# Building float32 weights from float64 words with integer operations, and a smaller feature pool, in a fused attention and MLP kernel

## The chip, the cores and the metric

The kernel runs on one core of a Trainium2 chip. The metric is the device time of one execution in microseconds (us); several runs are given by their median. The engines are TensorE (PE; PEld is its weight load), VectorE (DVE), ScalarE (ACT), GpSimd (POOL) and SyncE (SP), which here issues the DMA transfers. The notes call lines of the kernel `L95` and so on, by the kernel before.

## The reference

Three stages follow one another, on 8 batches of 576 rows with 512 features:

```python
kv = np.einsum('bhsd,bhse->bhde', k, v)                 # linear attention, 8 heads of 64
out = np.einsum('bhsd,bhde->bhse', q, kv)
x = out / np.sqrt(np.mean(out * out, -1, keepdims=True) + 1e-06) * g_norm

u = x + np.real(np.fft.fft(np.fft.fft(x, axis=1), axis=2))   # first MLP
un = (u - mean(u)) / np.sqrt(var(u) + 1e-06)
x = u + np.maximum(un @ w_ch1, 0.0) @ w_ch2                  # 512 -> 2048 -> 512

u = x + (x.T @ U @ V).T                                      # second MLP, rank 32
return u + np.maximum(u @ w_ch1, 0.0) @ w_ch2
```

The weights of both MLPs, and `U` and `V`, come as float64: 8 bytes an element, which the kernel reads as pairs of 32-bit words and turns into float32 on the chip.

## The kernel before

The 4608 rows are cut into 9 blocks of 512 (`NB`), and the 2048 hidden features into 16 groups of 128 (`NF`). One loop at the end of `tile_fused_kernel` runs over `n` from 0 to 287: steps 0 to 143 are the first MLP, 16 steps to a block, steps 144 to 287 the second. A step splits one tile of second-layer weights into a high and a low part (`split_w2`, `L153`, `L154`), does the first layer for one group (`emit_l1`, 12 matmuls, then `gh` on ScalarE and `gl` on VectorE, `L173`, `L174`), splits the first-layer weights of two steps later (`split_w1`, `L145`, `L146`), does the second layer for the group before (`emit_l2`, 12 matmuls), and then runs the side tasks that the table `side[n]` holds for it. The program order of each engine is written by hand in this way (`tc.manual_schedule()`); every engine, and SyncE's queue of transfers, executes in that order.

The side tasks of the first MLP's blocks are the attention, the Fourier transform and the normalisation of the next batch (`batch_tasks`, on all engines), loads, and the conversion of weights. A weight tile is 128x512 float64, loaded by `raw_load` (`L77`) into one of two buffers `raw` as 128x512x2 words: word 0 is the low half `lw`, word 1 the high half `hw` with sign, 11 bits of exponent and 20 of mantissa. `convert` takes a pair of tiles, `conv_a` for each and then `conv_b` for each:

- `conv_a`: VectorE masks the exponent out of `hw` into `pw` (`L85`), ScalarE scales and shifts it to a float32 exponent with `ebias` (`L86`) and scales the low words to float (`L87`), VectorE masks the mantissa with its leading one (`L88`).
- `conv_b`: VectorE puts the sign into `pw` (`L93`), and mantissa and low words together in floating point (`L95`); GpSimd multiplies by `pw` (`L97`).

After a pair, `w_next` issues the loads of the next pair into the two buffers. Three pairs of the first MLP's weights are converted ahead of the loop (two tiles of them one by one), the other 13 in steps 0 to 12 (`w_conv`), one in each. The second MLP's 16 pairs (`w_pre`) go to HBM as float32 and are read back later; they are converted in steps 0, 7 and 9 of blocks 1 to 5 and step 0 of block 6 (`spots`). The tables of `U` and `V` are converted in block 7 (`t_b_tables`), three tiles.

The features of a block are a pair of tiles `xh`, `xl` (high and low part), in pool `pa` for the first MLP, one buffer each, written by `t_tr`. For the second MLP `t_u2` writes them into pool `pb`, two buffers each, from step 10 of the block before. `pb` is opened in block 7 at the place of the attention's pool `at`, which is closed just before.

Of the kernel before, what the change touches and what calls it, by code (L numbers as in the profile page):

```python
# [10 lines left out]
F32 = mybir.dt.float32  # L11
F32R = mybir.dt.float32r
U32 = mybir.dt.uint32
AF = mybir.ActivationFunctionType
ALU = mybir.AluOpType
# [14 lines left out]
BT = 512  # L30
NB = NT // BT
NF = DFF // 128
VPAD = 192
EPS = 1e-6


@with_exitstack
def kernel(ctx: ExitStack, tc: tile.TileContext, qT, kvm, gn, w1a, w2a, w1b, w2b,
                      ucat, v4, tabs, outT):
    nc = tc.nc  # L40
    f32 = lambda ap: ap.bitcast(F32)

    com = ctx.enter_context(tc.tile_pool(name="com", bufs=1))
# [23 lines left out]
    ident = com.tile([128, 128], F32, name="ident")  # L67
    xe0 = com.tile([C, 3, B], F32, name="xe0")
    nhalf = com.tile([128, 8], F32, name="nhalf")
    ebias = com.tile([128, 1], F32, name="ebias")  # L70
    muT = com.tile([128, NT // 128], F32, name="muT")


    def raw_load(src, n):

        r = com.tile([128, 512, 2], U32, tag="raw", name="raw", bufs=2)
        nc.sync.dma_start(out=r[:, 0:n].rearrange("p n w -> p (n w)"), in_=src.bitcast(U32))  # L77
        return r[:, 0:n]

    def conv_a(raw, out):  # L80

        n = raw.shape[1]
        lw, hw = raw[:, :, 0], raw[:, :, 1]
        pw = com.tile([128, 512], U32, tag="cv1", name="cv1", bufs=2)[:, 0:n]
        nc.vector.tensor_scalar(out=pw, in0=hw, scalar1=0x7FF00000, scalar2=None, op0=ALU.bitwise_and)  # L85
        nc.scalar.activation(out=pw, in_=pw, func=AF.Relu, scale=8.0, bias=ebias)  # L86
        nc.scalar.activation(out=f32(lw), in_=lw, func=AF.Copy, scale=2.0 ** -52)  # L87
        nc.vector.tensor_scalar(out=out.bitcast(U32), in0=hw, scalar1=0xFFFFF, scalar2=0x100000,  # L88
                                op0=ALU.bitwise_and, op1=ALU.bitwise_or)
        return raw, out, pw  # L90

    def conv_b(raw, out, pw):
        nc.vector.scalar_tensor_tensor(out=pw, in0=raw[:, :, 1], scalar=0x80000000, in1=pw,  # L93
                                       op0=ALU.bitwise_and, op1=ALU.bitwise_or)
        nc.vector.scalar_tensor_tensor(out=out, in0=out.bitcast(U32), scalar=2.0 ** -20, in1=f32(raw[:, :, 0]),  # L95
                                       op0=ALU.mult, op1=ALU.add)
        nc.gpsimd.tensor_tensor(out=out, in0=out, in1=f32(pw), op=ALU.mult)  # L97

    def convert(*pairs):
        for c in [conv_a(*p) for p in pairs]:  # L100
            conv_b(*c)
# [56 lines left out]
    xt = {}  # L158
# [38 lines left out]
    pa = ctx.enter_context(tc.tile_pool(name="pa", bufs=1))  # L197
# [336 lines left out]
    pbx = {}  # L534
    x2 = {}
    pt = {}

    def t_b_tables(step):
        vw = S + 2 * VPAD
        half = [slice(0, vw // 2), slice(vw // 2, vw)]  # L540
        if step == 0:
            pbx["raw"] = [raw_load(ucat, 10 * RANK), raw_load(v4[:, half[0]], vw // 2)]
        elif step == 1:
            pb = pbx["pb"] = ctx.enter_context(tc.tile_pool(name="pb", bufs=1))
            uf = pb.tile([128, BT], F32, tag="o", name="uf", bufs=4)[:, 0:10 * RANK]
            convert((pbx["raw"].pop(0), uf))
            pbx["raw"].append(raw_load(v4[:, half[1]], vw // 2))
            uf = uf.rearrange("p (k r) -> p k r", r=RANK)
            u1 = pbx["u1"] = pb.tile([128, 10, 4, RANK], F32R, name="u1")
            for k in (0, 2, 3):  # L550
                nc.scalar.activation(out=u1[:, :, k, :], in_=uf, func=AF.Copy)
            nc.vector.tensor_tensor(out=u1[:, :, 1, :], in0=uf, in1=f32(u1[:, :, 0, :]), op=ALU.subtract)
        else:
            pb, c = pbx["pb"], half[step - 2]
            if step == 2:
                pbx["vs"] = pb.tile([128, vw], F32R, name="vs")
            vs = pbx["vs"]
            vf = pb.tile([128, BT], F32, tag="o", name="vf", bufs=4)[:, 0:vw // 2]
            convert((pbx["raw"].pop(0), vf))
            nc.scalar.activation(out=vs[:, c], in_=vf, func=AF.Copy)  # L560
            nc.vector.tensor_tensor(out=vs[96:128, c], in0=vf[96:128], in1=f32(vs[96:128, c]), op=ALU.subtract)
# [44 lines left out]
    def t_u2(j, dc):  # L606
        pb = pbx["pb"]
        blk = NB + j
        if dc == 0:
            xt[blk] = (pb.tile([128, 4, BT], F32R, tag="xh", name=f"xhb{j}", bufs=2),  # L610
                       pb.tile([128, 4, BT], F32R, tag="xl", name=f"xlb{j}", bufs=2))
        xh, xl = xt[blk]
        cols = slice(128 * dc, 128 * dc + 128)
        ps = side_bank(f"u2_{j}_{dc}")
# [60 lines left out]
    with tc.manual_schedule():  # L675
# [2 lines left out]
        nc.vector.memset(kvbd, 0.0)  # L678
        nc.vector.memset(f32(e288), 0.0)
        nc.scalar.activation(out=e288, in_=f32(e288), func=AF.Copy)  # L680
        nc.vector.memset(ebias, -896.0 * 2.0 ** 23)
        load_kv(0)
        load_q(0)
        nc.sync.dma_start(out=gnb, in_=gn)
# [33 lines left out]
        load_kv(1)  # L718
        t_s1(0, 0, 0)
        cv = [conv_a(raws.pop(0), w_new(0))]  # L720
        t_s1(0, 0, 1)
        t_s1(0, 1, 0)
        t_s1(0, 1, 1)
        conv_b(*cv[0])
        t_s2(0, 0)
        cv.append(conv_a(raws.pop(1), w_new(1)))
# [53 lines left out]
        for n in range(2 * NA):  # L780
            i, j = n % NF, n // NF
# [108 lines left out]
```

## Time and profile before

| | |
|---|---|
| runs | 1943.33 us (median of 3, 1941.99 to 1943.92) |
| the profiled execution | 1941.54 us, span 1939.7 us |
| PE busy | 1828.6 us, 94% |
| VectorE, ScalarE, GpSimd busy | 1000.8, 779.9, 769.0 us |
| TensorE's granted clock, mean | 0.976 |
| read from HBM, written | 102.88 MB, 36.73 MB |

The span runs from the first instruction to the last on the core. Busy times of different engines overlap. PE is full in the second half, so the place to look is the first: which engine PE waits for there, and what that engine does meanwhile. The chain of waits is followed back from the end: it shows in each moment one instruction or transfer without which the next could not have begun.

### The profile page before, as it was taken

What the parts mean: (1) busy time and instruction counts of PE and PEld (TensorE: products, weight loads), DVE (VectorE), ACT (ScalarE), POOL (GpSimd) and SP (SyncE); (2) the same over time, 40 slices, a digit from 0 to 9 for tenths busy, and PEclk for the clock granted to TensorE, in tenths of its full rate; (3) what the DMA queues carried; (4) which work ended last, traced back from release to release, by engine and by line L of the source; (5) the groups of instructions that cost most, each with busy time, mean ns of one, the idle gap of its engine ahead of it and who ended that gap; (6) DMA issues with size and microseconds to landing.
All of it is one profiled execution on the core that took longest, in us unless ns stands there. A gap on an engine that the chain in (4) does not pass through costs nothing.

```text
span 1939.7 us, 22822 instructions
## 1 busy us (share of the span) xinstructions
PE 1828.6 (94%) x8520; PEld 1509.4 (78%) x8520; DVE 1000.8 (52%) x1526; ACT 779.9 (40%) x1462; POOL 769.0 (40%) x592
## 2 busy tenths in 40 slices
PE   4667889999999999999999999999999999999999
PEld 3556778778787878878888888888888888888887
DVE  5898785766668576665443333333333333333222
ACT  4444443444434444433434343433343333333332
POOL 4586565544546554444322222232222222222322
PEclk7788999999999999999999999999999999999999
DMA  4524415133241513302222301010101010100000
GB/s 158 185 88 173 159 48 209 55 141 127 88 137 47 210 55 141 105 1 90 72 89 92 108 1 50 1 44 1 49 0 44 1 50 1 44 1 22 1 22 22
DMA packets 61760, 142.14 MB, mean 73 GB/s; under 512 B 11129, under 2 KB 13898, under 8 KB 58834
## 3 DMA queue, kind: packets, MB, share of 16 engines
q1 hardware_dynamic: 61650, 140.69, 20.9%
q8 instruction: 67, 1.10, 0.2%
q14 instruction: 43, 0.35, 0.1%
HBM read 102.88 MB, written 36.73 MB: 72 GB/s over the span
## 4 chain that ended last, share of the span: by engine, by line
PE 74%; DVE 13%; POOL 6%; issue 3%; ACT 3%; DMA 2%; SPq 0%; DVEq 0%; POOLq 0%; ACTq 0%
PE h L168 11%; PE h L170 11%; PE h L169 11%; PE acc L193 7%; PE acc L194 7%; PE acc L192 7%; PE acc L188 4%; PE acc L190 4%; PE acc L189 4%; POOL ss L269 2%; POOL x L282 2%; DVE f L301 2%; PE kv L244 2%; DVE eh L330 1%; DMA raw<-in_w2a 1%
## 5 line engine op out<-in xcount | busy, mean ns | idle before, releaser
L146 POOL TENSOR_TENSOR w1l<-w,w1h 128x512 fp32r<-128x512 f32 x274 | 357.0, 1303 | 972.1 <-ACT w1h L145 948.9
L174 DVE SCALAR_TENSOR_TENSOR gl<-h,gh 128x512 fp32r<-128x512 f32 x288 | 198.2, 688 | 392.4 <-ACT gh L173 392.2
L173 ACT ACTIVATE gh<-h 128x512 fp32r<-128x512 f32 x288 | 171.0, 594 | 501.8 <-PE h L170 501.7
L154 DVE TENSOR_TENSOR w2l<-w,w2h 128x512 fp32r<-128x512 f32 x283 | 208.7, 738 | 188.6 <-ACT w2h L153 187.8
L188 PE MATMUL acc<-w2h,gl 128*128 128x512 f32 x576 | 235.0, 408 | 47.4 <-DVE gl L174 47.4
L153 ACT ACTIVATE w2h<-w 128x512 fp32r<-128x512 f32 x288 | 180.9, 628 | 160.7 <-PE acc L194 113.0
L189 PE MATMUL acc<-w2l,gh 128*128 128x512 f32 x576 | 231.3, 402 | 6.6 <-POOL w2l L154 6.6
L168 PE MATMUL h<-xl,w1h 128*128 128x512 f32 x576 | 230.3, 400 | 1.4 <-DVE xl L492 1.4
L168 PE MATMUL h<-xlb,w1h 128*128 128x512 f32 x576 | 231.1, 401 | 0.0
L190 PE MATMUL acc<-w2h,gh 128*128 128x512 f32 x576 | 230.7, 401 | 0.0
L170 PE MATMUL h<-xh,w1l 128*128 128x512 f32 x576 | 226.4, 393 | 2.2 <-POOL w1l L146 2.2
L170 PE MATMUL h<-xhb,w1l 128*128 128x512 f32 x576 | 228.3, 396 | 0.0
L169 PE MATMUL h<-xhb,w1h 128*128 128x512 f32 x576 | 228.1, 396 | 0.0
L169 PE MATMUL h<-xh,w1h 128*128 128x512 f32 x576 | 225.9, 392 | 0.0
L194 PE MATMUL acc<-gh,w2h 128*128 128x512 f32 x576 | 225.4, 391 | 0.0
L193 PE MATMUL acc<-gl,w2h 128*128 128x512 f32 x576 | 225.4, 391 | 0.0
L192 PE MATMUL acc<-gh,w2l 128*128 128x512 f32 x576 | 224.7, 390 | 0.0
L145 ACT ACTIVATE w1h<-w 128x512 fp32r<-128x512 f32 x288 | 179.5, 623 | 22.9 <-POOL w L97 22.9
L188 PEld LDWEIGHTS acc<-w2h,gl 128*128 128x128 f32 x576 | 111.8, 194 | 80.0 <-DVE gl L174 57.4
L189 PEld LDWEIGHTS acc<-w2l,gh 128*128 128x128 f32 x576 | 112.2, 195 | 30.7 <-POOL w2l L154 8.2
L190 PEld LDWEIGHTS acc<-w2h,gh 128*128 128x128 f32 x576 | 112.0, 194 | 24.3
L170 PEld LDWEIGHTS h<-xh,w1l 128*128 128x128 f32 x576 | 109.2, 190 | 26.5 <-POOL w1l L146 2.6
(167 smaller groups left out, 2824.4 us busy)
## 6 DMA issues: line engine op xcount, KB each, us to landing
kv<-in_kvm SPq DMA_DIRECT2D x14, 1280.0 KB, 8.3
q<-in_qT SPq DMA_DIRECT2D x8, 1220.0 KB, 7.8
x_d<-x2o SPq DMA_DIRECT2D x36, 256.0 KB, 2.1
x2f<-x_d SPq DMA_DIRECT2D x36, 256.0 KB, 3.7
outT<-o SPq DMA_DIRECT2D x36, 256.0 KB, 2.0
raw<-in_w1a SPq DMA_DIRECT2D x16, 512.0 KB, 9.7
raw<-in_w2a SPq DMA_DIRECT2D x16, 512.0 KB, 3.5
u_d<-x SPq DMA_DIRECT2D x32, 256.0 KB, 2.6
```

The costliest lines, as they stand in the source:

```text
L146: (nc.vector if n in on_dve else nc.gpsimd).tensor_tensor(out=al, in0=a, in1=f32(ah), op=ALU.subtract)
L154: (nc.gpsimd if n in CLP else nc.vector).tensor_tensor(out=cl, in0=c, in1=f32(ch), op=ALU.subtract)
L168: nc.tensor.matmul(out=h, lhsT=ah[:, kc, :], rhs=xl[:, kc, :], start=(kc == 0), stop=False)
L169: nc.tensor.matmul(out=h, lhsT=ah[:, kc, :], rhs=xh[:, kc, :], start=False, stop=False)
L170: nc.tensor.matmul(out=h, lhsT=al[:, kc, :], rhs=xh[:, kc, :], start=False, stop=(kc == 3))
L174: nc.vector.scalar_tensor_tensor(out=gl, in0=h, scalar=0.0, in1=f32(gh), op0=ALU.max, op1=ALU.subtract)
L188: nc.tensor.matmul(out=a, lhsT=gl[:, tt], rhs=ch, start=s, stop=False)
L189: nc.tensor.matmul(out=a, lhsT=gh[:, tt], rhs=cl, start=False, stop=False)
L190: nc.tensor.matmul(out=a, lhsT=gh[:, tt], rhs=ch, start=False, stop=e)
L192: nc.tensor.matmul(out=a, lhsT=cl[:, tt], rhs=gh, start=s, stop=False)
L193: nc.tensor.matmul(out=a, lhsT=ch[:, tt], rhs=gl, start=False, stop=False)
L194: nc.tensor.matmul(out=a, lhsT=ch[:, tt], rhs=gh, start=False, stop=e)
```

## The change

`conv_a` and `conv_b` are rewritten. ScalarE now begins: it takes the absolute value of `hw`, read as a float32 (`Abs`), into `pw`; VectorE clamps it to the range that float32 can hold (`HMIN`, `HMAX`); ScalarE scales the low words by 2^-29 and writes them back as integers; VectorE shifts `pw` left by 3 and masks it, which gives exponent and upper mantissa bits of the result. `conv_b` is one VectorE instruction, which puts sign and top exponent bit of `hw` and the low words together, and an integer add on GpSimd in the multiply's place. The floating-point step `L95`, the constant `ebias` and its memset are gone.

The features of the second MLP's block `j` come from `x_new`: for odd `j` the tiles `xh`, `xl` of `pa`, for even `j` one buffer in `pb`, where the pair of block 0 is now the first thing allocated.

```diff
--- before.py
+++ after.py
@@ -33,6 +33,8 @@
 VPAD = 192
 EPS = 1e-6
 
+HMIN, HMAX = (float(v) for v in np.array([0x38000000, 0x47EFFFFF], np.uint32).view(np.float32))
+
 
 @with_exitstack
 def tile_fused_kernel(ctx: ExitStack, tc: tile.TileContext, qT, kvm, gn, w1a, w2a, w1b, w2b,
@@ -67,7 +69,6 @@
     ident = com.tile([128, 128], F32, name="ident")
     xe0 = com.tile([C, 3, B], F32, name="xe0")
     nhalf = com.tile([128, 8], F32, name="nhalf")
-    ebias = com.tile([128, 1], F32, name="ebias")
     muT = com.tile([128, NT // 128], F32, name="muT")
 
 
@@ -79,22 +80,22 @@
 
     def conv_a(raw, out):
 
+
+
         n = raw.shape[1]
         lw, hw = raw[:, :, 0], raw[:, :, 1]
         pw = com.tile([128, 512], U32, tag="cv1", name="cv1", bufs=2)[:, 0:n]
-        nc.vector.tensor_scalar(out=pw, in0=hw, scalar1=0x7FF00000, scalar2=None, op0=ALU.bitwise_and)
-        nc.scalar.activation(out=pw, in_=pw, func=AF.Relu, scale=8.0, bias=ebias)
-        nc.scalar.activation(out=f32(lw), in_=lw, func=AF.Copy, scale=2.0 ** -52)
-        nc.vector.tensor_scalar(out=out.bitcast(U32), in0=hw, scalar1=0xFFFFF, scalar2=0x100000,
-                                op0=ALU.bitwise_and, op1=ALU.bitwise_or)
+        nc.scalar.activation(out=f32(pw), in_=f32(hw), func=AF.Abs)
+        nc.vector.tensor_scalar(out=f32(pw), in0=f32(pw), scalar1=HMIN, scalar2=HMAX, op0=ALU.max, op1=ALU.min)
+        nc.scalar.activation(out=lw, in_=lw, func=AF.Copy, scale=2.0 ** -29)
+        nc.vector.tensor_scalar(out=out.bitcast(U32), in0=pw, scalar1=3, scalar2=0x3FFFFFF8,
+                                op0=ALU.logical_shift_left, op1=ALU.bitwise_and)
         return raw, out, pw
 
     def conv_b(raw, out, pw):
-        nc.vector.scalar_tensor_tensor(out=pw, in0=raw[:, :, 1], scalar=0x80000000, in1=pw,
+        nc.vector.scalar_tensor_tensor(out=pw, in0=raw[:, :, 1], scalar=0xC0000000, in1=raw[:, :, 0],
                                        op0=ALU.bitwise_and, op1=ALU.bitwise_or)
-        nc.vector.scalar_tensor_tensor(out=out, in0=out.bitcast(U32), scalar=2.0 ** -20, in1=f32(raw[:, :, 0]),
-                                       op0=ALU.mult, op1=ALU.add)
-        nc.gpsimd.tensor_tensor(out=out, in0=out, in1=f32(pw), op=ALU.mult)
+        nc.gpsimd.tensor_tensor(out=out.bitcast(U32), in0=out.bitcast(U32), in1=pw, op=ALU.add)
 
     def convert(*pairs):
         for c in [conv_a(*p) for p in pairs]:
@@ -535,6 +536,10 @@
     x2 = {}
     pt = {}
 
+    def x_new(j):
+        pool = pa if j % 2 else pbx["pb"]
+        return tuple(pool.tile([128, 4, BT], F32R, tag=t, name=f"{t}b{j}") for t in ("xh", "xl"))
+
     def t_b_tables(step):
         vw = S + 2 * VPAD
         half = [slice(0, vw // 2), slice(vw // 2, vw)]
@@ -542,6 +547,7 @@
             pbx["raw"] = [raw_load(ucat, 10 * RANK), raw_load(v4[:, half[0]], vw // 2)]
         elif step == 1:
             pb = pbx["pb"] = ctx.enter_context(tc.tile_pool(name="pb", bufs=1))
+            xt[NB] = x_new(0)
             uf = pb.tile([128, BT], F32, tag="o", name="uf", bufs=4)[:, 0:10 * RANK]
             convert((pbx["raw"].pop(0), uf))
             pbx["raw"].append(raw_load(v4[:, half[1]], vw // 2))
@@ -606,9 +612,8 @@
     def t_u2(j, dc):
         pb = pbx["pb"]
         blk = NB + j
-        if dc == 0:
-            xt[blk] = (pb.tile([128, 4, BT], F32R, tag="xh", name=f"xhb{j}", bufs=2),
-                       pb.tile([128, 4, BT], F32R, tag="xl", name=f"xlb{j}", bufs=2))
+        if dc == 0 and j:
+            xt[blk] = x_new(j)
         xh, xl = xt[blk]
         cols = slice(128 * dc, 128 * dc + 128)
         ps = side_bank(f"u2_{j}_{dc}")
@@ -678,7 +683,6 @@
         nc.vector.memset(kvbd, 0.0)
         nc.vector.memset(f32(e288), 0.0)
         nc.scalar.activation(out=e288, in_=f32(e288), func=AF.Copy)
-        nc.vector.memset(ebias, -896.0 * 2.0 ** 23)
         load_kv(0)
         load_q(0)
         nc.sync.dma_start(out=gnb, in_=gn)
```

On VectorE, at step 0 of block 0, the first pair of the loop reads before (`w2l` and `gl` are the step's low parts, `cv` is `pw`, `w` the result):

```order
L95 SCALAR_TENSOR_TENSOR w_0_2_594<-w_0_2_594,raw 128x512
L154 TENSOR_TENSOR w2l_616<-w_0_0_415,w2h_615 128x512
L174 SCALAR_TENSOR_TENSOR gl_633<-h_619,gh_632 128x512
L85 TENSOR_SCALAR cv_642<-raw 128x512
L88 TENSOR_SCALAR w_0_3_640<-raw 128x512
L85 TENSOR_SCALAR cv_647<-raw 128x512
L88 TENSOR_SCALAR w_0_3_641<-raw 128x512
L93 SCALAR_TENSOR_TENSOR cv_642<-raw,cv_642 128x512
L95 SCALAR_TENSOR_TENSOR w_0_3_640<-w_0_3_640,raw 128x512
L93 SCALAR_TENSOR_TENSOR cv_647<-raw,cv_647 128x512
L95 SCALAR_TENSOR_TENSOR w_0_3_641<-w_0_3_641,raw 128x512
L154 TENSOR_TENSOR w2l_663<-w_0_1_485,w2h_662 128x512
```

and with the change, on the same engine at the same place:

```order
L155 TENSOR_TENSOR w2l_608<-w_0_0_412,w2h_607 128x512
L175 SCALAR_TENSOR_TENSOR gl_625<-h_611,gh_624 128x512
L89 TENSOR_SCALAR cv_634<-cv_634 128x512
L91 TENSOR_SCALAR w_0_3_632<-cv_634 128x512
L89 TENSOR_SCALAR cv_639<-cv_639 128x512
L91 TENSOR_SCALAR w_0_3_633<-cv_639 128x512
L96 SCALAR_TENSOR_TENSOR cv_634<-raw 128x512
L96 SCALAR_TENSOR_TENSOR cv_639<-raw 128x512
L155 TENSOR_TENSOR w2l_653<-w_0_1_481,w2h_652 128x512
```

The pair has six instructions in place of eight; the first of each tile now reads `cv`, ScalarE's result, and no longer `raw`.

On ScalarE, at the same place, before:

```order
L153 ACTIVATE w2h_615<-w_0_0_415 128x512
L173 ACTIVATE gh_632<-h_619 128x512
L145 ACTIVATE w1h_636<-w_0_2_593 128x512
L86 ACTIVATE cv_642<-cv_642,ebias 128x512
L87 ACTIVATE raw<-raw 128x512
L86 ACTIVATE cv_647<-cv_647,ebias 128x512
L153 ACTIVATE w2h_662<-w_0_1_485 128x512
```

and with the change:

```order
L154 ACTIVATE w2h_607<-w_0_0_412 128x512
L174 ACTIVATE gh_624<-h_611 128x512
L146 ACTIVATE w1h_628<-w_0_2_587 128x512
L88 ACTIVATE cv_634<-raw 128x512
L90 ACTIVATE raw<-raw 128x512
L88 ACTIVATE cv_639<-raw 128x512
L154 ACTIVATE w2h_652<-w_0_1_481 128x512
```

The places are the same; the first activation of each tile reads `raw`, the loaded words, where it read VectorE's result, and it stands behind `gh` and `w1h` in the queue. On GpSimd, SyncE and PE the order is the same row for row.

## Rows read from the trace of the kernel before

**Rows 1.** The page's first line
```profile
span 1939.7 us, 22822 instructions
```

**Rows 2.** Stretches: us, length, then busy time of each engine, clock, DMA
```profile
84.00:240.00 156.00, 120.60 (x534) 95.85 (x533) 132.19 (x194) 72.36 (x136) 108.55 (x72) 0.90 0.40 140
130.00:140.00 10.00, 4.35 (x11) 2.83 (x10) 8.39 (x9) 5.13 (x9) 6.56 (x6) 0.67 0.33 105
240.00:900.00 660.00, 632.80 (x3167) 533.43 (x3166) 451.11 (x700) 285.64 (x570) 344.00 (x270) 0.99 0.30 105
300.00:350.00 50.00, 50.00 (x266) 42.62 (x265) 29.48 (x49) 17.93 (x34) 22.67 (x23) 1.00 0.43 149
900.00:1939.70 1039.70, 1035.83 (x4597) 844.08 (x4595) 357.99 (x532) 386.43 (x674) 277.50 (x216) 1.00 0.10 34
```

**Rows 3.** PE's waits from 240 to 900 us: total, times, longest
```profile
PE acc L188 <- DVE gl L174: 27.2, 14, 2.3
```

**Rows 4.** The chain from 44 to 240 us: shares by line; start, length
```profile
by line: DMA raw<-in_w2a 13.0%; DVE w L95 10.9%; issue 9.9%; DVE cv L93 5.4%; DVE cv L85 5.1%; POOL w L97 4.6%; POOL x L282 4.3%; DVE eh L330 2.9%; POOL ss L269 2.8%; POOL x L383 2.4%; PE tr L487 2.3%; DVE w L88 2.3%; DVE f L301 2.3%; DVE g
...
64.09 1.67 DVE w L95
...
198.96 1.67 DVE w L95
```

**Rows 5.** The conversion by tile and by line: ns min/median/max, first and last start
```profile
L85 DVE TENSOR_SCALAR cv<-raw x67: 399/420/1510, 44.9 to 957.9; 128x512 uint32<-128x512 uint32 x64, 128x480 uint32<-128x480 uint32 x2, 128x320 uint32<-128x320 uint32 x1
L86 ACT ACTIVATE cv<-cv,ebias x67: 563/723/729, 45.9 to 958.3; 128x512 uint32<-128x512 uint32 x64, 128x480 uint32<-128x480 uint32 x2, 128x320 uint32<-128x320 uint32 x1
L93 DVE SCALAR_TENSOR_TENSOR cv<-raw,cv x67: 492/682/1224, 48.6 to 959.7; 128x512 uint32<-128x512 uint32 x64, 128x480 uint32<-128x480 uint32 x2, 128x320 uint32<-128x320 uint32 x1
L97 POOL TENSOR_TENSOR w<-w,cv x32: 1259/1642/2881, 50.0 to 221.1; 128x512 f32<-128x512 f32 x32
...
L95 DVE SCALAR_TENSOR_TENSOR w<-w,raw x32: 673/685/1785, 49.2 to 219.2; 128x512 f32<-128x512 uint32 x32
```

**Rows 6.** VectorE in order of time: start, length
```profile
97.33 1.77 DVE L95 SCALAR_TENSOR_TENSOR w<-w,raw 128x512 f32<-128x512 uint32 x1
...
108.71 1.75 DVE L154 TENSOR_TENSOR w2l<-w,w2h 128x512 fp32r<-128x512 f32 x1
...
114.92 0.42 DVE L85 TENSOR_SCALAR cv<-raw 128x512 uint32<-128x512 uint32 x1
...
117.47 0.68 DVE L93 SCALAR_TENSOR_TENSOR cv<-raw,cv 128x512 uint32<-128x512 uint32 x1
118.08 0.68 DVE L95 SCALAR_TENSOR_TENSOR w<-w,raw 128x512 f32<-128x512 uint32 x1
```

**Rows 7.** GpSimd in order of time, the same stretch
```profile
97.05 1.50 POOL L97 TENSOR_TENSOR w<-w,cv 128x512 f32<-128x512 f32 x1
...
113.23 7.25 POOL L282 TENSOR_TENSOR x<-x,gnb 128x512 f32<-128x512 f32 x2
```

**Rows 8.** Who subtracts for w2l from 84 to 240 us
```profile
L154 DVE TENSOR_TENSOR w2l<-w,w2h x11: 676/679/1745, 90.3 to 237.5; 128x512 fp32r<-128x512 f32 x11
```

**Rows 9.** The chain at the start of block 1
```profile
246.48 0.39 DVE wpre L95
...
247.68 0.75 DVE wpre L95
248.43 0.86 issue
```

**Rows 10.** Who waits around the tile of the exponents: us, times
```profile
  ACT cv L86: 63.6, 42
...
  DVE cv L93: 4.7, 4
```

**Rows 11.** Two other GpSimd operations: ns min/median/max
```profile
L637 POOL TENSOR_TENSOR o<-xhb,xlb x36: 1274/1287/1752, 1161.8 to 1923.0; 128x512 f32<-128x512 f32 x36
...
L269 POOL TENSOR_TENSOR ss<-ss,nhalf x40: 1629/1918/2158, 17.0 to 828.5; 128x8 f32<-128x8 f32 x32, 98x8 f32<-98x8 f32 x8
```

## The prediction

> **What bounds the kernel now.** I read the stretches first. From 900 us on PE is busy 1035.8 of 1039.7 us at full clock, so nothing the other engines save there can show; between 240 and 900 us it stands idle for 27 us, between 84 and 240 us (the first MLP's block 0) for 35 us, and there the granted clock averages 0.90 [rows 2]. The waits say for whom: between 240 and 900 us the second layer's first matmul waits 14 times for `gl` from VectorE, 27.2 us, which is all of that idle time [rows 3]. So VectorE's place in the step is what can be bought. The chain from 44 to 240 us then says which VectorE work: `L95`, the last step of the weight conversion, holds 10.9% of 196 us, 21.4 us, more than any other instruction; the multiply after it on GpSimd (`L97`) holds 4.6%, 9.0 us; the loads of raw words hold 13.0%, 25 us [rows 4]. The conversions left for block 0 are 13 pairs, one in each of the steps 0 to 12.
>
> What one conversion costs: `L85` and `L88` 0.42 us each, `L93` 0.68, `L95` 0.685 at the median but 1.785 at worst, `L97` 1.64 at the median and 1.26 at best [rows 5]. The stretched ones explain themselves in the order of time. The second `L95` of a pair takes 1.77 us where it starts 0.28 us behind `L97`, and so does a `w2l` subtraction (1.75) that stands there instead [rows 6, 7]. The other way round, eight conversion instructions from 114.92 us on run at 0.42 and 0.68 us while two GpSimd multiplies beside them take 7.25 us [rows 6, 7]. So these instructions exclude one another: what one engine gives up, the other can use.
>
> **What the change takes out.** 67 instructions `L95`, one per conversion, and nothing comes in their place: the exponent is now put together by shifts and an integer add. VectorE's busy time should fall by at least 67 x 0.685, 46 us, and by more for the stretched ones; only a part of that is on the path.
>
> *Block 0 and the start.* All of `L95`'s 21.4 us on the chain is the upper end. Seven of its pieces there are stretched ones, about 1.7 us each (the first and the last in [rows 4]), some 1.08 above 0.60, the pitch at which two such instructions follow each other (117.47 and 118.08 us [rows 6]). That excess belongs to the multiply, which still runs, and meets whatever comes next. In block 0 this is a `w2l` subtraction on VectorE in 11 of 16 steps [rows 8], which is excluded too; in the other 5 GpSimd makes `w2l` itself and VectorE goes on with `gl` out of PSUM. So 11/16 of 7 x 1.08, 5.2 us, is only handed on: 21.4 - 5.2 = **16.2 us**, lower end 21.4 - 7.6 = 13.8.
>
> The Trainium skill (SBUF — State Buffer, Who interferes with whom) calls this pair of ports an exclusive lock that the first comer keeps for its whole instruction. By that rule every stretched piece is handed on and the sum takes 13.8; the trace agrees where VectorE is late [rows 6], but shows GpSimd stretched far beyond one VectorE instruction [rows 7], so the order of issue does not settle it.
>
> *GpSimd.* The integer add is not in the trace. Nearest is the float add of the same tile, 1.287 us [rows 11]; farthest is the power, 1.918 us for 8 columns, which shows that an operation of another kind can cost a multiple per element [rows 11]. I take 1.29. With one excluded VectorE instruction fewer, `L97`'s 9.0 us on the chain shrink by 1 - 1.29/1.64: **1.9 us**, lower end 0.
>
> *Blocks 1 to 6.* Each has a pair (second MLP's weights) in its first step, where VectorE has just caught up with PE: in block 1 `L95` holds 0.39 and 0.75 us of the chain, and 0.86 us of issue stands behind [rows 9]. Then follow normalisation, folds and the idle PE. I take two pitches of 0.60, 1.2 us a block, 6 x 1.2 = **7.2 us**; ends 1.14 and 2.0, 6.8 and 12 us. The other ten of these pairs stand at steps 7 and 9, where PE is busy 50 of 50 us [rows 2]: 0. The conversions of the tables lie behind 900 us: 0, and if that cover went, 3 x 0.7 us.
>
> **What it moves.** Before, VectorE began a conversion as soon as the words had landed, and ScalarE waited for it. Now ScalarE begins (absolute value) and VectorE's clamp waits. Behind that clamp stand `w2l` and `gl`, and behind them PE. ScalarE is the early one today: it waited 63.6 us in 42 places for `L85`, and VectorE 4.7 us in 4 for ScalarE [rows 10]. Where the words come last, VectorE starts one activation later (`L86`, 0.72 us [rows 5]), but no longer waits for it in the middle. I charge **1.5 us**; the ends are 0 and 0.6 us for each of 19 pairs, 11 us. The clamp, the shift and the new OR are priced like `L85`, `L88` and `L93`, the same kinds on the same widths; if the clamp ran like `L93`, 0.26 us more, 19 pairs would lose 10 us, which lies inside the range. Order and number of instructions on GpSimd, SyncE and PE are unchanged; each raw load waits for the last reader of its buffer, now the OR, one instruction earlier.
>
> *The pools.* Odd blocks' features of the second MLP go to the first MLP's buffers, whose last reader is block 8, eleven steps before the first write; two buffers still alternate. Dropping `ebias` takes one memset away. Both: 0, covered by the saturated PE [rows 2].
>
> **Sum.** 16.2 + 1.9 + 7.2 - 1.5 = 23.8 us. The profiled execution took 1941.54 us for its span of 1939.7 [rows 1]; 1941.5 - 23.8 = 1917.7, and the median of the runs lies 1.8 above that execution: **1919 us**. What is late next is the raw loads, 25 us of the chain, which stay.
>
> **Rivals.**
> 1. *The integer add is slow.* GpSimd runs it by another loop. A pair frees two VectorE slots of 0.6 us; an add longer than 1.29 + 0.6 = 1.9 us takes them back, and from there the kernel is slower. At 2.6 us, twice the float add, a pair loses 1.4 us: 19 x 1.4 = 27 us, of which GpSimd's idle third in block 0 (108.5 busy of 156 [rows 2]) hides 9: 1961. For it: the power's price [rows 11], and no integer add in the trace. Against it: all 128x512 two-input operations on GpSimd cost about 1.26 to 1.29 at best, whatever the operation [rows 5, 11]. Chance 0.09. The Trainium skill (GPSIMD Engine Reference, Engine selection) says only that such an add is done natively and exactly, and gives no price.
> 2. *The new wait eats it.* ScalarE's queue is in order, and the absolute value stands behind `gh` and the high parts, which wait for PE and GpSimd. If that makes the clamp late by 0.6 us in each of 19 pairs, and the raw loads hold the chain in a third of block 0 (5 of the 16 us), the gain is 23.8 - 10 - 5, some 8 us: 1935; with the clamp's worse price, nothing. For it: 13% of raw loads on the chain [rows 4]. Against: 63.6 against 4.7 us [rows 10]. Chance 0.14, of which 0.06 ends within 0.2%.
> 3. *More comes back.* If all stretched pieces go, 21.4 + 1.9 + 12, and the clock of block 0 rises: it is 0.90 over 156 us, 0.67 (between the levels of 1.2 and 2.4 GHz) where PE works 4.35 of 10 us, and 1.00 where it is always busy [rows 2], so a busier PE may get back some of the 16 us that 0.10 lacks: 40 us and more, 1900 or below. For it: PE idles 62 us from 84 to 900 us. Against: the loads, and that GpSimd is nearly as full as VectorE. Chance 0.06.
>
> **The numbers.** Forecast 0.71: a gain of 10 us (13.8 + 0 + 6.8 - 11) to 35 us (21.4 + 1.9 + 12 - 0), 1908 to 1933. The range leaves out most of rivals 1 and 3 and the end of rival 2: 1899 to 1940. A measurement tells 0.2%, 4 us, from no change. Faster 0.71 + 0.06 + 0.08 = 0.85; same 0.06, and 0.01 from rival 1; slower 0.08.
>
> **What would show it.** Right: VectorE's busy time down by 46 us or more; the new OR at 0.68 us and hardly stretched, `w2l` stretched more often; the add at 1.3 us or a little above; the wait for `gl` between 240 and 900 us at about 20 instead of 27 us; block 8 reached some 24 us earlier, and the same time from there to the end. Wrong: the add near 2 us or more; long waits of the clamp for ScalarE; the clamp at 0.7 us; or PE idle in block 0 as before, with the raw loads in `L95`'s place on the chain.

## The result

The changed kernel takes **1920.11 us** (median of 4 runs, 1918.78 to 1920.98); the kernel before took 1942.66 us beside it (4 runs, 1941.12 to 1943.92). The ratio is 0.9884, with an interval of 0.9867 to 0.9901: 1.2% faster, 22.5 us, where the prediction said 1919 us. The profiled execution took 1920.98 us for a span of 1919.2, 20.6 us less than the one of before. The total came out within 1 us; two of its terms did not, and a third that was put at nothing had a value. They are taken apart below.

The page of the kernel after, its first lines (busy us, share of the span, instructions):

```profile
span 1919.2 us, 22748 instructions
## 1 busy us (share of the span) xinstructions
PE 1816.7 (95%) x8520; PEld 1504.9 (78%) x8520; DVE 966.8 (50%) x1458; ACT 773.9 (40%) x1462; POOL 751.5 (39%) x592
```

VectorE is busy 34 us less than before (1000.8), not 46 or more: what `L95` gave up, other instructions took over in part; `w2l` alone went from 208.7 to 231.8 us. The stretches, cut where block 0 and the long stall now end (us, length; busy time of PE, PEld, DVE, ACT, POOL; granted clock, DMA share, GB/s), against [rows 2]:

```profile
84.00:228.80 144.80, 116.42 (x533) 93.98 (x532) 116.92 (x166) 69.67 (x136) 96.09 (x70) 0.91 0.41 148
228.80:900.00 671.20, 644.74 (x3235) 542.51 (x3234) 447.69 (x682) 286.95 (x579) 341.73 (x272) 0.99 0.30 104
900.00:1919.20 1019.20, 1014.67 (x4522) 830.98 (x4520) 346.37 (x514) 380.56 (x665) 273.84 (x214) 1.00 0.10 34
```

Block 0 and the start are shorter, PE idles in the blocks from 1 on for about as long as before (26.5 us), and behind 900 us, where nothing should have changed, PE is as full as ever and the stretch is 20.5 us shorter. Of these 15.3 are only that block 7 begins sooner (900.1 us instead of 915.4); the other 5 are a gain of that stretch itself.

The conversion by tile and line (ns min/median/max, first and last start; then who waited around that tile), against [rows 5, 10]. `L88` is the absolute value, `L89` the clamp, `L91` the shift, `L96` the OR, `L98` the integer add:

```profile
L88 ACT ACTIVATE cv<-raw x67: 490/666/708, 45.1 to 942.3; 128x512 f32<-128x512 f32 x64, 128x480 f32<-128x480 f32 x2, 128x320 f32<-128x320 f32 x1
L89 DVE TENSOR_SCALAR cv<-cv x67: 407/428/1519, 45.8 to 943.0; 128x512 f32<-128x512 f32 x64, 128x480 f32<-128x480 f32 x2, 128x320 f32<-128x320 f32 x1
L96 DVE SCALAR_TENSOR_TENSOR cv<-raw x67: 493/684/1121, 48.1 to 944.7; 128x512 uint32<-128x512 uint32 x64, 128x480 uint32<-128x480 uint32 x2, 128x320 uint32<-128x320 uint32 x1
...
L98 POOL TENSOR_TENSOR w<-w,cv x32: 1259/1660/1751, 48.8 to 208.7; 128x512 uint32<-128x512 uint32 x32
...
  ACT w1h L146: 35.5, 14
...
  DVE cv L89: 19.5, 23
```

Each instruction costs what its neighbour in the old trace cost: the integer add 1.26 us at best and 1.66 at the median, the multiply 1.26 and 1.64. The wait is new: VectorE's clamp waited for ScalarE 23 times, 19.5 us, where its waits around this tile had been 4.7 us in 4.

And the excess of a pair, some 1.08 us on VectorE beside GpSimd's operation, went on to the next instruction. VectorE at the start of block 1, in order of time (start, length), in the kernel after:

```profile
232.20 0.42 DVE L89 TENSOR_SCALAR cv<-cv 128x512 f32<-128x512 f32 x1
232.65 0.43 DVE L91 TENSOR_SCALAR wpre<-cv 128x512 uint32<-128x512 uint32 x1
233.00 0.42 DVE L89 TENSOR_SCALAR cv<-cv 128x512 f32<-128x512 f32 x1
233.45 0.43 DVE L91 TENSOR_SCALAR wpre<-cv 128x512 uint32<-128x512 uint32 x1
233.80 1.29 DVE L96 SCALAR_TENSOR_TENSOR cv<-raw 128x512 uint32<-128x512 uint32 x2
235.00 1.76 DVE L155 TENSOR_TENSOR w2l<-w,w2h 128x512 fp32r<-128x512 f32 x1
236.68 0.68 DVE L175 SCALAR_TENSOR_TENSOR gl<-h,gh 128x512 fp32r<-128x512 f32 x1
```

and the same place before:

```profile
244.44 0.42 DVE L85 TENSOR_SCALAR cv<-raw 128x512 uint32<-128x512 uint32 x1
244.78 0.42 DVE L88 TENSOR_SCALAR wpre<-raw 128x512 uint32<-128x512 uint32 x1
...
247.60 1.76 DVE L95 SCALAR_TENSOR_TENSOR wpre<-wpre,raw 128x512 f32<-128x512 uint32 x1
249.29 0.68 DVE L154 TENSOR_TENSOR w2l<-w,w2h 128x512 fp32r<-128x512 f32 x1
```

Before, the stretched instruction was `L95` (1.76 us) and `w2l` behind it ran at 0.68; now `w2l` is stretched to 1.76. From the pair's first instruction to `gl` it is 4.48 us instead of 5.45 (`gl` started at 249.89): 0.97 us saved.

Where the time went, from the starts of each block's first `gl` in the traces (us; 80.7 and 82.0 are the first of all; "odd" are blocks 1, 3, 5, 7 of the second MLP, whose features went to the first MLP's pair, "even" its blocks 0, 2, 4, 6):

```
                before   after  gain   predicted
to step 0         82.0    80.7   1.3   } 17.1
block 0          159.1   148.1  11.0   }
blocks 1-6       674.3   671.2   3.1     6.7
blocks 7-8       182.8   182.8   0.0     0
2nd MLP, odd     374.6   369.2   5.4     0
2nd MLP, even    377.9   377.5   0.4     0
last block+end    89.0    89.7  -0.6     0
```

(The predicted 1.5 us for the wait is split here by its 13 and 6 pairs.) In this pair of traces block 0 and the start gave 5 us less than forecast, blocks 1 to 6 gave 3.6 less, and the second MLP's blocks gave 6 that nobody had counted. The first of these is the least certain, as experiment 2 will show.

### The profile page after: what moved, and what is told of

It reads as the page before. It is cut to its first block, busy times and chain, and to the rows that moved or that the text cites. A ratio compares the mean times of both kernels' runs of the same rounds, so it can differ in the third digit from the quotient of the medians.

```text
span 1919.2 us, 22748 instructions
## 1 busy us (share of the span) xinstructions
PE 1816.7 (95%) x8520; PEld 1504.9 (78%) x8520; DVE 966.8 (50%) x1458; ACT 773.9 (40%) x1462; POOL 751.5 (39%) x592
## 4 chain that ended last, share of the span: by engine, by line
PE 81%; DVE 9%; POOL 4%; ACT 3%; issue 2%; DMA 1%; SPq 0%; DVEq 0%; POOLq 0%; ACTq 0%
PE h L169 12%; PE h L171 12%; PE h L170 12%; PE acc L195 7%; PE acc L194 7%; PE acc L193 7%; PE acc L189 5%; PE acc L191 5%; PE acc L190 5%; DVE f L302 2%; PE kv L245 2%; DVE eh L331 1%; POOL ss L270 1%; PE o L263 1%; PE pt L603 1%
## 5 line engine op out<-in xcount | busy, mean ns | idle before, releaser
L155 DVE TENSOR_TENSOR w2l<-w,w2h 128x512 fp32r<-128x512 f32 x283 | 231.8, 819 | 188.6 <-ACT w2h L154 187.8
L146 ACT ACTIVATE w1h<-w 128x512 fp32r<-128x512 f32 x288 | 179.9, 625 | 35.5 <-POOL w L98 35.5
L169 PEld LDWEIGHTS h<-xlb,w1h 128*128 128x128 f32 x576 | 108.3, 188 | 25.5 <-issue 2.6
```

Source lines behind the costliest of these rows:

```text
L155: (nc.gpsimd if n in CLP else nc.vector).tensor_tensor(out=cl, in0=c, in1=f32(ch), op=ALU.subtract)
L169: nc.tensor.matmul(out=h, lhsT=ah[:, kc, :], rhs=xl[:, kc, :], start=(kc == 0), stop=False)
```

## The experiments

The theory after the result: (a) the pools are worth the 5.8 us, by the place of the features and nothing else; (b) in block 0 the change frees more than was forecast, and the new wait for ScalarE takes back several times the 1.5 us charged. Rivals: the 5.8 us come from the conversion or from a displaced table; and block 0 falls short because the add holds VectorE up as long as the multiply did.

**1. The new conversion with the old pools.**

```diff
-            xt[NB] = x_new(0)
...
-        if dc == 0 and j:
-            xt[blk] = x_new(j)
+        if dc == 0:
+            xt[blk] = (pb.tile([128, 4, BT], F32R, tag="xh", name=f"xhb{j}", bufs=2),
+                       pb.tile([128, 4, BT], F32R, tag="xl", name=f"xlb{j}", bufs=2))
```

> The changed kernel with the pools of the kernel before (both feature pairs of the second MLP in pb). Theory 'place': the 6 us that the changed kernel gained behind step 144 come from where the features lie, and the conversion alone is worth what block 0 and blocks 1 to 6 show, 15 us: 1926 us, and all blocks of the second MLP take 94.5 us again, with a first-layer matmul every 234 ns. Rival 'conversion': the gain behind step 144 has to do with the conversion or the clock, and the pools are worth nothing, as I forecast: 1920 us, odd blocks 93.1 us.

Measured: 1926.39 us (1923.58 to 1927.19), ratio 0.9916 (0.9901 to 0.993). The odd blocks take 374.6 us again, as before the change.

**2. The old conversion with the new pools**, the opposite half.

> The kernel before with the changed pools alone. Theory 'place': 1942.7 - 5.9 = 1937 us; blocks j = 1, 3, 5, 7 of the second MLP 93.1 us at 227 ns a first-layer matmul, the even ones 94.4 at 234, the first MLP unchanged. Rival 'conversion': 1942.7 us, all blocks 94.5.

Measured: 1936.47 us, ratio 0.997 (0.9961 to 0.9979). The odd blocks take 369.2 us as in the full change, and blocks 1 to 6 stay at 673.9. The halves add up: 16.3 us and 6.2 us, together the 22.5 of the change. The conversion has nothing to do with the second MLP's gain.

Block 0 executes the instructions of the kernel before, and yet took 161.9 us where it had taken 159.1. PE worked longer at a lower granted clock, in the old trace and in this one (columns as above):

```profile
82.00:241.10 159.10, 123.70 (x551) 98.55 (x550) 133.30 (x197) 73.67 (x139) 110.55 (x73) 0.90 0.41 140
82.10:244.00 161.90, 126.21 (x544) 99.95 (x544) 131.93 (x197) 73.91 (x139) 111.31 (x73) 0.87 0.40 138
```

So one trace of block 0 is good to some 3 us: with the old conversion it ends at 241.1 and 244.0 us, with the new one (the change and experiments 1, 3 and 4) between 227.7 and 229.5. What block 0 and the start fell short by is 1 to 5.5 us, according to the pair of traces; by the medians of experiment 1, 16.3 us where 23.8 were forecast, less the 3.6 of blocks 1 to 6, it is about 4, an estimate.

The trace shows what differs in the second MLP. Three matmuls of one step, kernel after, in an odd block (start, length; the first is one of the first layer's, the second is the second layer's first, the third comes three matmuls behind that):

```profile
1199.93 0.39 PE L171 MATMUL h<-xhb,w1l 128*128 128x512 f32 x1
...
1201.52 0.39 PE L193 MATMUL acc<-gh,w2l 128*128 128x512 f32 x1
...
1202.20 0.39 PE L193 MATMUL acc<-gh,w2l 128*128 128x512 f32 x1
```

and in an even one:

```profile
1299.90 0.39 PE L171 MATMUL h<-xhb,w1l 128*128 128x512 f32 x1
...
1301.54 0.39 PE L193 MATMUL acc<-gh,w2l 128*128 128x512 f32 x1
...
1302.24 0.39 PE L193 MATMUL acc<-gh,w2l 128*128 128x512 f32 x1
```

From the first row's start to the second's it is seven matmuls: 1.59 us, 227 ns each, and 1.64 us, 234 ns each. Both blocks run at full clock with PE hardly ever idle, and the instructions are the same. What differs is where the 512 columns are read from: by the built program's allocation the pair of the odd blocks lies at bytes 106400 to 122784 of a partition, that of the even blocks from byte 143424 up (before, both pairs from 191328 up). An odd block gained 1.36 us, four of them the 5.4 us in the table. Not all of it falls on the matmuls that read the features: in the median of its steps the twelve first-layer matmuls went from 2.806 to 2.749 us, which is 0.9 us in 16 steps, and the second layer's start right behind them was late as well (0.70 instead of 0.68 us for three matmuls in the rows above), though it reads `gh` and `gl` at the same bytes in both blocks. Why the delay runs on into them no run here shows.

**3. The even blocks' pair put low as well**: the high parts in the four buffers of `un` (up to byte 130976) and the low parts in the two of `raw`, none of which is used any more by then. `Cols` lets the rest of the kernel address such pieces as one tile. All else is as in the change.

```diff
+        return (Cols([pa.tile([128, BT], F32R, tag="un", name=f"xhb{j}_{t}", bufs=4) for t in range(4)], 1),
+                Cols([com.tile([128, 2, BT], F32R, tag="raw", name=f"xlb{j}_{t}", bufs=2) for t in range(2)], 2))
```

> The changed kernel with the even pair in two other places that are idle in the second MLP: xh in the four buffers of the first MLP's rows (bytes 122784 to 130976 of a partition by the allocation), xl in the two buffers of raw words (4000 to 12192). Theory 'low bytes': a feature tile is read slower where it lies high in the partition, with a border between 122784 and 143424; all blocks of the second MLP then run at 227 ns, j = 0, 2, 4, 6 take 93.1 instead of 94.4 us and j = 8 79.2 instead of 80.4: 1920.1 - 6.5 = 1913.6 us. Rival 'neighbours': what matters is whether the pair shares the pool with the tiles that are written and read meanwhile, or that one pair stands apart from the other; then nothing or part of it comes: 1917 to 1920.

Measured: **1911.44 us** (1910.13 to 1912.96), ratio 0.9839 (0.9823 to 0.9855), the fastest version with the whole computation in this study. The four even blocks take 372.2 us instead of 377.5, the odd ones 368.8, and the last block, even too, 78.9 instead of 80.4. The page says it in one line, PE's busy time down by 7 us with as many matmuls:

```profile
PE 1809.5 (95%) x8520; PEld 1504.4 (79%) x8520; DVE 967.4 (51%) x1458; ACT 774.1 (41%) x1462; POOL 752.7 (39%) x592
```

**4. The opposite: the first pair moved up**, by allocating `pa`'s other tiles ahead of it, so that it lies at bytes 127040 to 143424, its low parts from 135232.

> The changed kernel with the same tiles in pool pa, in another order: rows, residuals and outputs first, so that the first pair moves from bytes 106400 to 122784 up to 127040 to 143424 (xh to 135232, xl above). Theory 'low bytes' with a border at 131072: matmuls on xl take 234 ns each in all blocks, those on the last two quarters of xh too, those on its first quarter 227; blocks 7 and 8 of the first MLP and the odd blocks of the second lose 0.9 to 1 us each, the stalled blocks less: 1926 to 1931 us. Rival 'neighbours' (the pool and its other tiles matter, not the bytes): 227 ns as before, 1920 us.

Measured, one run: 1929.35 us. Blocks 7 and 8 of the first MLP, whose features no other edit of this study moved, go from 182.8 to 185.8 us, and the odd blocks back to 374.6: 234 ns for each first-layer matmul. So it is not the pool and not the second MLP, but the place within the partition. Nor is it the alignment: before the change all of this lay 32 bytes higher, `xh` at byte 106432, and blocks 7 and 8 took 182.8 us there too, though 106432 is a multiple of 64 and not of 128, as the slow 127040 and 143424 are. Places up to byte 130976 (experiment 3) are fast, a pair that reaches from 127040 to 143424 is slow, and so is all that was tried higher up. If there is one border, it lies between 127040 and 143424; which part of this pair is already slow the timing does not tell.

**5. Without the absolute value**: the clamp reads the loaded words, sign included.

```diff
-        nc.scalar.activation(out=f32(pw), in_=f32(hw), func=AF.Abs)
-        nc.vector.tensor_scalar(out=f32(pw), in0=f32(pw), scalar1=HMIN, scalar2=HMAX, op0=ALU.max, op1=ALU.min)
+        nc.vector.tensor_scalar(out=f32(pw), in0=f32(hw), scalar1=HMIN, scalar2=HMAX, op0=ALU.max, op1=ALU.min)
```

> The changed kernel without the absolute value: the clamp reads the high words as they are, so negative weights come out wrong; the 67 activations and VectorE's wait for them are gone. Theory 'new wait' (my rival 2: the clamp comes late because ScalarE must act first; 19.5 us of such waits in 23 places, and the activation holds 5.5% of the chain from 44 to 240 us, 10.8 us): block 0 ends 6 to 10 us earlier, 1910 to 1914 us. Theory 'port' (what is missing in block 0 is handed on to the next VectorE instruction that shares GpSimd's port): 1 to 3 us, 1917 to 1919 us, and the w2l subtraction behind a pair still takes 1.75 us.

Measured: 1910.98 us, ratio 0.9839 (0.982 to 0.9859). Block 0 takes 141.5 us instead of 148.1 and its first step begins 1.7 us earlier: together 8.3 us, and `w2l` is as stretched as ever (1.76 us at the median from 75 to 220 us). So the wait and the activation that causes it cost **8.3 us** in block 0 and the start, give or take the 1 us by which that stretch differs among the traces with the new conversion.

**6. Without the add on GpSimd.**

> The changed kernel without GpSimd's integer add, so that the sign, the top exponent bit and the low bits of every weight are missing. Theory 'port': the w2l subtraction behind a pair falls from 1.75 to 0.68 us, a pair gets 1.1 us shorter on VectorE, GpSimd loses 3 us a pair; block 0 gains 13 x 1.1 = 14 us or more, blocks 1 to 6 some 1.1 us each, 6 us: 1900 us or below. Theory 'new wait': the clamp still waits for ScalarE and the chain hardly changes: 1915 us.

Measured: 1897.96 us, ratio 0.9772 (0.9753 to 0.9792). Block 0 takes 134.7 us, 13.4 less than after, and blocks 1 to 6 take 7.7 us less. `w2l` on VectorE in block 0, of the kernel after and of this one (ns min/median/max):

```profile
L155 DVE TENSOR_TENSOR w2l<-w,w2h x12: 679/1763/1789, 79.0 to 225.2; 128x512 fp32r<-128x512 f32 x12
```

```profile
L154 DVE TENSOR_TENSOR w2l<-w,w2h x12: 674/682/1157, 78.9 to 210.7; 128x512 fp32r<-128x512 f32 x12
```

1.08 us each, as forecast for a stretched piece, and gone with the add. Both halves of the theory are real: the wait, and the stretch that GpSimd's operation causes. The 13.4 us are not the price of the stretch alone, since GpSimd's own 1.66 us a tile are gone too, and with them the 35.5 us in which `w1h` waited for the add.

**7. The activations of a pair interleaved**: both absolute values, then both copies, and the clamps ahead of the shifts, to shorten the wait.

```diff
...
+    def conv_s(*cs):
+        for raw, out, pw in cs:
+            lw = raw[:, :, 0]
+            nc.scalar.activation(out=lw, in_=lw, func=AF.Copy, scale=2.0 ** -29)
+        for raw, out, pw in cs:
+            nc.vector.tensor_scalar(out=out.bitcast(U32), in0=pw, scalar1=3, scalar2=0x3FFFFFF8,
+                                    op0=ALU.logical_shift_left, op1=ALU.bitwise_and)
...
```

> The changed kernel with the two tiles of a pair interleaved: both absolute values first on ScalarE, both clamps before both shifts on VectorE. A shift that follows its own clamp starts 0.46 us after it, one instruction after another without such a dependence 0.34; a pair has two such places. If these 0.11 us lie on the path: 0.22 x 19 pairs, 4 us, and some of the clamp's wait: 1914 to 1917 us. If they are hidden, 1920 us; if the second clamp's earlier need for ScalarE hurts, above.

Measured: 1921.11 us (1918.19 to 1921.62), ratio 0.9892 (0.9876 to 0.9909): no difference from the change. Blocks without the low clock described below take 111.6 instead of 111.9 us: a shift that does not follow its own clamp directly starts 0.34 us behind it, one that does 0.45. In block 0 the clamps waited longer for ScalarE, from 75 to 235 us 20.1 us in 12 places, against 13.7 us in 13 in the kernel after.

**8. Experiments 3 and 7 together.**

> Both: even pair in the low places of low_even (1911.4 us) and interleaved pairs. If the two add up: 1905 to 1909 us.

Measured: 1914.10 us (1912.37 to 1915.09), ratio 0.9854 (0.984 to 0.9869). Missed: no better than experiment 3 alone.

**9. ScalarE's part of a pair put ahead of the step's other tasks**, so that VectorE should find it done; the even blocks' high parts low, their low parts high at byte 191296.

```diff
+            side[n].insert(0, lambda m=m: w_begin(m, m + 1))
+            side[n].append(lambda m=m: w_conv(m, m + 1))
...
+            side[spots[k]].insert(0, lambda m=m: w_begin(m, m + 1))
             side[spots[k]].append(lambda m=m: w_pre(m, m + 1))
```

> The changed kernel with ScalarE's two activations of each tile of a pair moved to the front of the step's side tasks, ahead of the attention's copies for which ScalarE waits; and, in the second MLP only, the even pair's xh in the low place of low_even (122784 to 130976) with xl left in pool pb (191296 and up). First part: if the 8.4 us that the absolute value costs until block 1 are VectorE's waits for a late ScalarE, most of them come back: block 0 ends 4 to 7 us earlier than in the changed kernel, and the clamp's waits (19.5 us in 23 places) fall below 8 us. If they are ScalarE's load as such, or the early activation now holds up ScalarE behind the raw words' transfers, nothing comes or time is lost. Second part, 'low bytes': a matmul is slow when its own moving tile lies high, so in even blocks those on xl are slow and those on xh fast: a block takes about 93.1 + 1.35/3 = 93.6 us. If one high tile slows the whole group: 94.4. In all: 1912 to 1916 us.

Measured: 1945.19 us (1943.7 to 1946.35), ratio 1.0016 (1.0007 to 1.0025): 25 us slower than the change and about 30 off the expectation. The edit did what it was to do, since VectorE's clamp now waits 5.7 us instead of 17.3 for the absolute value up to the end of block 0, and yet block 0 takes 163.4 us. The chain of waits from 44 us to the end of block 0 says why; of the kernel after:

```profile
by line: issue 6.8%; DMA raw<-in_w1a 6.8%; ACT cv L88 5.9%; POOL w L98 5.8%; DVE cv L89 5.7%; DVE w L91 5.1%; DVE cv L96 5.1%; DMA raw<-in_w2a 3.9%; POOL ss L270 3.4%; DVE f L302 3.1%; DVE w2l L155 3.1%; DVE eh L331 3.0%; PE tr L488 2.5%; D
```

and of this one:

```profile
by line: DMA raw<-in_w1a 14.7%; DMA raw<-in_w2a 14.2%; ACT cv L85 7.0%; issue 6.7%; DVE cv L97 5.6%; ACT raw L86 5.2%; DVE cv L103 5.2%; DVE w L98 4.2%; PE tr L495 2.3%; DVE un L485 1.7%; DVE ln L479 1.3%; PE acc L196 1.3%; PE acc L197 1.2%
```

The loads of raw words hold 28.9% of 199 us, 57 us, where they held 10.7% of 185 us, 20 us. In order of time:

```profile
197.58 0.33 SPq L78 DMA_DIRECT2D raw<-in_w1a  x1
...
201.14 0.66 ACT L85 ACTIVATE cv<-raw 128x512 f32<-128x512 f32 x1 [1.25 <-DMA raw<-in_w1a]
...
203.49 0.25 ACT L256 ACTIVATE kvbd<-kv 64x128 f32<-64x128 f32 x1
203.78 0.29 DVE L257 COPY kvbd<-kv 64x128 f32<-64x128 f32 x1 [3.40 <-ACT kvbd L256]
```

A load is issued when the OR has read its buffer, lands 3.6 us later, and ScalarE, whose queue is in order, stands at the absolute value until then. What it had done in that time before (`kvbd`, `de`, `w2h`, `gh`) now comes behind four activations, and VectorE waits for that instead. The load had been hidden under ScalarE's other work, and the edit took the cover away.

In blocks 1 to 6, 9.8 us longer than after the change, it is another wait. Loads hardly count there; but the four activations, 2.2 us, stand in the blocks' first step ahead of `sq`, the squares that the next batch's normalisation needs, and VectorE waits for these, in block 1:

```profile
246.27 0.69 DVE L275 TENSOR_REDUCE ss<-sq 128x8 f32<-128x512 f32 x1 [1.35 <-ACT sq L272]
```

PE's wait for `gl` there is 34.3 us instead of 26.5, which is most of the 9.8.

The second part of the edit: with the high parts low and the low parts high, the even blocks of the second MLP take 377.0 us, against 377.5 with both high and 372.2 with both low. Of three matmuls in a row two now read low addresses, and the twelve of a step take 2.795 us, nearly the 2.806 of both high and not the 2.749 of both low: one high tile slows the others' matmuls as well.

**10. The same with both features of the even blocks low.**

> The same early activations, with the even pair wholly in the low places of low_even (1911.4 us). If the early activations give 4 to 7 us in block 0: 1904 to 1908 us, the fastest of all that compute the reference. If they give nothing: 1911 us.

Measured: 1936.91 us (1933.38 to 1937.48), ratio 0.997 (0.9957 to 0.9982): 8.3 us less than experiment 9, which is the low pair again, and 25 more than experiment 3. Missed for the same reason.

## Why the prediction was right, and where its terms were not

The forecast case came (faster, conversion shortened, GpSimd's add no dearer), and the range held it. That the time is only 1 us off is luck: in the traces two terms were too large by some 9 us together, and one that stood at zero brought 6.

- *The bound.* Right. The gain lies where VectorE is late, and `gl` still rules the stalls behind block 0. The forecast 20 us for PE's wait did not show: 27.2 us [rows 3] became 26.5, from 228 to 885 us:

```profile
PE acc L189 <- DVE gl L175: 26.5, 18, 2.3
```

  By blocks the sum hides two things. PE's waits in block 1 and in block 4 before, and in block 1 after:

```profile
PE acc L188 <- DVE gl L174: 5.4, 3, 2.3
PE acc L188 <- DVE gl L174: 4.1, 2, 2.3
PE acc L189 <- DVE gl L175: 4.4, 3, 2.2
```

  Block 1's stall shrank by the 1.0 us that VectorE saved. In blocks 3 to 6 before it was only 4.1 us, which goes with a stretch at low clock ahead of a later stall (shown below for block 4). After, PE waits 4.4 us in blocks 3 and 5 and runs them at full clock, and what they gain is its busy time (108.8 to 107.5 us).

- *Block 0 and the start, 16.2 and GpSimd's 1.9.* Without the absolute value the same stretch gains 20.6 us over before, 12.2 + 8.3; that is what the removal is worth, if one counts the lost activation with it. The 18.1 forecast was 2.5 too small (5.4 by the trace of experiment 2). Handing on was right: `w2l` took the stretch over (1.763 us median, and 0.682 without the add). The Trainium skill (SBUF — State Buffer, Who interferes with whom) has an instruction with two SBUF inputs on VectorE contend with GpSimd's reads, whichever issues first holding the ports; the 12 `w2l` rows agree. By that rule every stretched piece is handed on, and the term would have been its lower end, 13.8: the stretch lost none of its 1.08 us, but the sum came out above both values. How GpSimd's own 1.9 us fared cannot be told apart: the add has the multiply's price, 1.66 against 1.64 us.

- *The new wait, 1.5 us.* **This is the step that failed.** It was priced by the waits of the old trace, 63.6 against 4.7 us [rows 10], on the ground that ScalarE is the early one. In that trace ScalarE waited for VectorE, because VectorE began; made to begin itself, it comes when its queue lets it. The five longest of the clamp's waits in block 0 are 11.7 us together. Two of them stand behind a load (1.58 and 3.48 us), the other three behind ScalarE's earlier tasks for the next batch. One of each kind, kernel after:

```profile
122.19 0.63 ACT L285 ACTIVATE x<-x 34x512 f32<-34x512 f32 x1 [2.47 <-POOL x L283]
122.84 0.66 ACT L88 ACTIVATE cv<-raw 128x512 f32<-128x512 f32 x1
123.61 0.43 DVE L89 TENSOR_SCALAR cv<-cv 128x512 f32<-128x512 f32 x1 [2.81 <-ACT cv L88]
...
168.52 0.66 ACT L88 ACTIVATE cv<-raw 128x512 f32<-128x512 f32 x1 [3.21 <-DMA raw<-in_w1a]
169.28 0.43 DVE L89 TENSOR_SCALAR cv<-cv 128x512 f32<-128x512 f32 x1 [3.48 <-ACT cv L88]
```

  Experiment 5 gives 8.3 us in block 0 and the start, inside the bound of 11. Rival 2 had the mechanism right, ScalarE's queue and the loads, and its size nearly, though not what the absolute value would stand behind; that the kernel still gained is due to the removal being worth more and to the pools.

- *Blocks 1 to 6, 7.2 us.* 1.2 us a block was charged and 0.97 measured on VectorE in block 1, since a shift right behind its own clamp starts 0.45 us after it, not 0.34: 2 x 0.11 per pair. Blocks 1, 2, 3 and 5 gained 1.0 us each. Blocks 4 and 6 lost half a us instead, and with them goes the clock. The stretches of the kernel after around 610 us, in block 4 (columns as above):

```profile
605.00:610.20 5.20, 3.10 (x14) 2.25 (x12) 2.67 (x6) 3.39 (x8) 0.15 (x1) 1.00 0.00 0
610.20:613.70 3.50, 3.34 (x8) 2.67 (x9) 2.66 (x6) 2.00 (x5) 1.12 (x1) 0.51 0.01 2
613.70:617.00 3.30, 3.30 (x23) 3.08 (x22) 1.65 (x3) 1.29 (x3) 1.29 (x1) 1.00 0.87 295
...
625.00:640.00 15.00, 15.00 (x79) 12.92 (x78) 9.88 (x16) 6.53 (x13) 8.39 (x9) 1.00 0.39 140
```

  and of before, in its block 4:

```profile
606.00:612.30 6.30, 3.96 (x18) 2.99 (x17) 3.58 (x5) 2.77 (x6) 3.28 (x4) 1.00 0.00 0
612.30:615.80 3.50, 3.50 (x9) 2.75 (x9) 3.47 (x5) 0.42 (x1) 2.20 (x2) 0.51 0.00 0
...
620.00:630.00 10.00, 8.29 (x38) 6.63 (x37) 6.62 (x11) 5.82 (x14) 2.38 (x2) 1.00 0.01 2
```

  Each time PE has idled some 2 us for `gl`, and then runs for 3.5 us at 0.51, the level of 1.2 GHz. Before, another stall follows in the same block (8.29 of 10 us busy), which would only have been longer (5.4 us in block 1, 4.1 here): blocks 3 to 5 take 112.9 us each, as block 1, which has no such stretch. After, it comes behind the block's last stall, PE is full from there on, and blocks 2 and 4 take 113.5 us where 1, 3 and 5 take 111.9. Other versions pay in other blocks: four of them in experiment 1, two in experiment 3. What decides it was not tried.

- *The pools, 0.* **The second step that failed**: "0, covered by the saturated PE". A saturated PE covers what other engines do, but not what makes its own instructions longer. Experiments 1 and 2 show 5.4 to 6.2 us, and experiment 3 shows 6.8 more for the pair that the change left high (even blocks 5.3, last block 1.5).

- *Behind 900 us.* Apart from that nothing: blocks 7 and 8 take 182.8 us in both. Rival 1 did not come, since the integer add runs at the float price. Rival 3 would have needed the chain's loads to go, and 20 us of them are left.

## What to carry to other kernels

When an edit moves the first step of a chain to another engine, price the wait by where that step stands in the new engine's queue (what it is behind, and when its data land), not by who waited for whom while the order was another; and moving it ahead is no cure if it then waits for a load that other work used to cover. A saturated engine hides the work of the others, but not a change in its own operands: look at the pitch of the same instruction in different blocks, and at the addresses. And a forecast that comes out should be checked term by term, since here 9 us and 6 us of opposite errors cancelled for the most part.

## What the hardware showed that was not expected

- A first-layer matmul of 512 columns is followed by the next after 227 to 228 ns where its moving operand, the features, lies below byte 130976 of a partition, and after 233 to 234 ns, 3% more, where the pair of features lies from 143424 up or reaches from 127040 to there (medians of each block, in all twelve traces). With one tile of the pair low and one high a step's twelve matmuls take 2.795 us, between 2.749 and 2.806 and near the latter.
- The second-layer matmuls right behind a slow group are late too, by 14 to 24 ns over a step's twelve, though their own operands did not move.
- A shift on VectorE that reads the result of the clamp right ahead of it started 0.45 us after it, an independent instruction of the same kind 0.34 to 0.35 (128x512).
- GpSimd's 32-bit integer add has the price of the float multiply at each width: at best 1.26 us for 512 columns, 1.22 against 1.23 for 480, 0.87 against 0.89 for 320.
